# Attention with a relative bias and a snake MoE layer: two shared PSUM banks, MoE blocks entered inside a head pair, and a new order

## The chip, the cores and the metric

The kernel runs on one core of a Trainium2 chip. Its engines are TensorE (PE in the profile: matmuls and transposes, with PEld for the loading of weights), VectorE (DVE), ScalarE (ACT: exponentials and sines), GpSimd (POOL: here it issues loads that change the type from float32 to float16) and SyncE (SP: it issues transposing and plain transfers). Each engine works through its own list of instructions in order; an instruction waits until what it needs is there, and everything behind it on that engine waits too. The metric is device time in microseconds; lower is better.

## The reference

Batch element by batch element (8), head by head (8), over 576 positions with 64 numbers a head:

```python
scores = scale * q @ k.T  + bias_table[bucket(|i - j|)]
attn   = exp(scores - max) ; attn = attn / (sum(attn) + 1e-9)
x      = (attn @ v), heads side by side          # 4608 tokens x 512
h      = x @ w_in                                # 4608 x 2048
g      = h + sin(alpha * h) ** 2 / (alpha + 1e-9)
out    = g @ w_out                               # 4608 x 512, float32
```

The bias depends only on the distance of two positions and is constant from distance 128 on.

## The kernel before, in words

**Attention.** An element's heads are taken in four pairs (`attn_pair`). Scores are made transposed, keys on partitions. A pair has five tiles of 128 x 1024 in PSUM, each of two banks: one "X" tile for the last 64 keys and the last 64 queries, and four "T" tiles, named T(element).(pair).(w)(half), for 256 keys by 256 queries of both heads. For elements 0 and 1 an "S" tile follows after pair 1; from element 2 on it comes first, and it holds the last 64 keys against the last 64 queries of all heads. ScalarE takes the exponential of each tile into `u` (L567, some 0.94 us each); VectorE multiplies a band by a mask of exponentials of the bias (`band`, `band_x`, L736 to L744, L659, L661), since the bias is a constant outside the band. The numerators and the denominators come from matmuls of `u` with `v` and a column of ones (`av_task`, L680, L684): two groups per pair, the first of two, the second of three units. `norm` (L694, L695) divides into `xp`, and a transposing transfer on SyncE's queue (L775) writes `xT`, features on partitions.

**MoE.** The 4608 tokens are taken in nine blocks of 512 (`moe_in`). A block has eight parts `in b.d` (L800: eight matmuls of 512 columns each into a two-bank tile), each followed by two sines on ScalarE (L810), a square (L817) and two fused products on VectorE (L824), which read the tile again and write `g`. Then come four output tiles `mo b.a` (L857), each of four pieces of four matmuls that add up in one bank, an eviction on VectorE (`ev`, L873) and a store.

**PSUM.** The eight banks are three two-bank tiles `big` for scores and MoE parts, one bank `av` for numerators and the small masks, and one bank `mo` for the MoE outputs and for the transposes of keys and queries. Only the last two blocks put every second output into `av`.

**Masks.** The mask matrix `m2` has three blocks of 128 columns per head; `mask` makes each by 64 small matmuls (L476) and an exponential (L480). `masks_tail` makes `mt` from it.

**Loads.** Keys and queries of elements 0 and 1 come by GpSimd in their natural layout and are transposed by TensorE (`load_nat`, `turn`, L400 and L394): element 0 in runs of six rows, element 1 in `natural_chunk` loads, 128 positions of all heads each, with a tail. From element 2 on they are staged in DRAM as float16 (L242), transposed on SyncE's queue (L249), and the last 64 keys are put into `kL` (L433), which `S` and `X` tiles use. GpSimd's queue holds, for element 1: keys and queries, `w_in`, `v`, `w_out`.

**Order.** No order is written down: every piece of work is a task with an engine, a planned duration, what it depends on, rings of buffers and a priority; `_Plan.run` steps through planned time and emits, whenever an engine is free, the ready task with the lowest priority number. The planned times decide nothing but the order in which instructions stand on each engine; on the chip semaphores hold. Score tiles go in batches of two; `"big"` and `"ACT"` are sequences in the order of the code, so where `moe_in` is called decides where a block's parts stand among the scores: for element t, block t - 1 is called after pair 1. The output pieces `mo` fill in between (priority 2).

Of the kernel before, what the change touches and what calls it, by code (L numbers as in the profile page):

```python
# [25 lines left out]
class _Ring:  # L26
# [6 lines left out]
    def can(self, k):  # L33
# [11 lines left out]
        return end  # L45

# [14 lines left out]
class _Plan:  # L61
# [46 lines left out]
    def run(self):  # L108
# [9 lines left out]
        while left:  # L118
            moved = False
            nxt = None  # L120
            for e, lst in engs.items():
# [13 lines left out]
                if best is not None:  # L135
# [8 lines left out]
                    for ring, users in best.rings:  # L144
                        ring.users.append(users)
# [11 lines left out]
        return order  # L157


@with_exitstack  # L160
def kernel(
# [11 lines left out]
    nc = tc.nc  # L173
# [26 lines left out]
    for g in range(4):  # L200
# [31 lines left out]
    big, avr, mor = _Ring(3), _Ring(1), _Ring(1)  # L232
    ur, usr, sr, sqr, gr, xr, outr, rr = (
        _Ring(NU), _Ring(2), _Ring(NS), _Ring(NS), _Ring(NG), _Ring(NX), _Ring(NO), _Ring(4))

# [38 lines left out]
    def natural_chunk(src, t, kind, c):  # L274

        def emit():
            nc.gpsimd.dma_start(
                out=rows_of(t)[:, 5 * kind + c, :].rearrange("p (h d) -> p h d", d=D),
                in_=bass.AP(tensor=src.tensor, offset=src.offset + t * H * S * D + 128 * c * D,
                            ap=[[D, 128], [S * D, H], [1, D]]))  # L280
        return emit
# [89 lines left out]

    T_kT = [[None] * NP for _ in range(T)]
# [7 lines left out]
    def turn(t, p):  # L380

        for kind in range(2):
# [3 lines left out]
            def e_pe(kind=kind, cell=cell, first=first):  # L386

                bank = "av" if first else "mo"
                s = cell["t"] = ps.tile([128, 512], F32, name=bank, tag=bank, bufs=1).bitcast(F16)
# [17 lines left out]
            def e_cp(kind=kind, cell=cell, first=first):  # L407
# [7 lines left out]
                else:  # L415
                    nc.vector.tensor_copy(out=dst, in_=src)
            users = []
            a = add("PE", 0.6, e_pe, deps=T_nat[t][p][kind] + [t_sp0], prio=-0.5 if t else -2 if p == 0 else 0,
                    rings=[(avr, users)] if first else [(mor, users)], mode="full",
                    name=f"turn{t}.{p}.{kind}")  # L420
# [19 lines left out]
    def load_nat(t):  # L440
# [3 lines left out]
        def one(emit, dur, lat):  # L444
            first = not made
            made.append(add("GQ", dur, emit, lat=lat, seq="GQ",
                            rings=[(gr, nat_users[t])] if first else []))
            return made[-1]
        if t == 0:
            for h0, n, lat in ((0, 2, 4.0), (2, 2, 5.0), (4, 4, 6.0)):  # L450
                got = [[one(natural(src, t, kind, h0, n), 0.5 * n, lat)] for kind, src in kq]
                for p in range(h0 // 2, (h0 + n) // 2):
                    T_nat[t][p] = got
        else:
            got = [[one(natural_tail(src, t, kind), 0.7, 4.0)] for kind, src in kq]
            for kind, src in kq:
                got[kind] += [one(natural_chunk(src, t, kind, c), 0.9, 5.0) for c in range(4)]
            for p in range(NP):
                T_nat[t][p] = got

    load_nat(0)
    T_v[0] = add("GQ", 5.0, load_v(0), deps=[t_dve0], lat=6.0, seq="GQ")

# [29 lines left out]

    T_mt = []
    t_al = add("SP", 0.5, pre_sp2, deps=T_m2, lat=6.0)
    t_alpha = add("DVE", 0.4, pre_alpha, deps=[t_al])

    def masks_tail():

        for pp in range(2):  # L500
            cell = {}

            def g_mm(pp=pp, cell=cell):
                av = ps.tile([128, 512], F32, name="av", tag="av", bufs=1)
# [8 lines left out]
            def g_cp(pp=pp, cell=cell):  # L513
# [3 lines left out]
            a = add("PE", 0.4, g_mm, deps=list(T_m2), prio=-1, rings=[(avr, users)],  # L517
                    mode="full")
            b = add("DVE", 0.5, g_cp, deps=[a], prio=-1, name=f"mt.{pp}")
# [7 lines left out]
    def later_loads(t):  # L527
        pre_k = last_qk[t - 2] if t >= 2 else []
        pre_v = last_av[t - 2] if t >= 2 else [t_dve0]
        def w_ins():  # L530
            for j in range(4):
                T_win.append(add("GQ", 2.5, w_in_load(j), lat=6.0, seq="GQ"))

        def kqs():
            if t < TN:
                load_nat(t)
                return
            a = add("GQ", 4.0, stage(k, staged_k, t), lat=2.5, seq="GQ")
            b = add("GQ", 4.0, stage(q, staged_q, t), lat=2.5, seq="GQ")
# [7 lines left out]
        def v_s():  # L547
            T_v[t] = add("GQ", 5.0, load_v(t), deps=pre_v, lat=3.0, seq="GQ")

        def w_outs():  # L550
            for i in range(4):
                T_wout.append(add("GQ", 2.5, w_out_load(i), lat=6.0, seq="GQ"))
# [398 lines left out]
```

## Time and profile before

| what | us |
| --- | --- |
| median of three runs (406.03, 407.64, 407.49) | 407.49 |
| the profiled execution's own time | 406.59 |
| its span, from the first to the last instruction | 404.6 |
| TensorE busy | 375.5 |
| VectorE busy | 289.5 |
| ScalarE busy | 270.1 |
| GpSimd busy | 82.6 |
| mean granted TensorE clock | 0.987 of full |

The profile shows one execution. A line of the timeline gives the start, the busy time, the engine, the source line, the operation with its tiles, how many instructions were merged, and in brackets the idle time of that engine before it with what ended it. A line of waits gives who waited for whom: the total, how often, the longest. In the stretches, the columns are the length and the busy time of each engine with its number of instructions, then the granted clock.

### The profile page before, as it was taken

The page shows a single profiled execution, that of the slowest core. Times are in us where ns is not written, and L with a number is a line of the kernel's source. Part 1 is how long each engine was busy: PE and PEld are TensorE (multiplying, and loading weights), DVE is VectorE, ACT ScalarE, POOL GpSimd, SP SyncE. Part 2 cuts the span into 40 slices and gives each one's busy share as a digit, 9 for nine tenths or more (in the row PEclk, how much of TensorE's full clock was granted, in tenths as well). Part 3 has the DMA queues.
Part 4 walks back from the last instruction along what each step waited for, and adds up shares of the span by engine and source line. Part 5 has one row for each costly group of instructions (what it writes and reads, how often), then busy time and mean ns, then how long its engine had stood idle before and what let it go on. Part 6 is the DMA issues. An engine that isn't in the chain of part 4 may idle for free.

```text
span 404.6 us, 9103 instructions
## 1 busy us (share of the span) xinstructions
PE 375.5 (93%) x3816; PEld 202.9 (50%) x3816; DVE 289.5 (72%) x618; ACT 270.1 (67%) x333; POOL 82.6 (20%) x88
## 2 busy tenths in 40 slices
PE   6788599989999999999999999999999998999996
PEld 5465353555446554555456545654565454444442
DVE  4587469666976698659956896779666964699811
ACT  4688656977588847895788668866888583566200
POOL 8772634053002600080008000400000000000000
PEclk9699899999999999999999999999999999999999
DMA  9999999999933998199919991981021103000121
GB/s 128 137 180 159 168 178 158 157 161 156 145 82 57 153 154 110 45 145 140 132 56 114 150 139 56 113 145 42 28 64 40 32 38 86 26 0 2 52 79 78
DMA packets 167180, 41.27 MB, mean 102 GB/s; under 512 B 158308, under 2 KB 162020, under 8 KB 167140
## 3 DMA queue, kind: packets, MB, share of 16 engines
q0 software_dynamic: 106816, 18.36, 60.9%
q1 hardware_dynamic: 60180, 22.17, 31.7%
q8 instruction: 30, 0.49, 0.5%
q10 hardware_dynamic: 144, 0.17, 0.2%
q14 instruction: 10, 0.08, 0.1%
HBM read 36.88 MB, written 16.52 MB: 132 GB/s over the span
## 4 chain that ended last, share of the span: by engine, by line
PE 49%; DVE 25%; DMA 11%; ACT 10%; issue 5%; SPq 0%; POOL 0%; ACTq 0%; DVEq 0%; POOLq 0%
PE mo L857 20%; DVE g L824 11%; PE big L800 11%; DMA xT<-xp 8%; ACT u L567 7%; DVE sq L817 5%; PE av L684 5%; PE big L725 3%; PE av L857 3%; DVE outs L873 3%; DVE xp L695 2%; ACT s L810 2%; DMA kL<-kT 2%; DVE u L736 2%; PE av L680 1%
## 5 line engine op out<-in xcount | busy, mean ns | idle before, releaser
L567 ACT ACTIVATE u<-big 128x1024 f16<-128x1024 f32 x160 | 153.3, 1026 | 32.2 <-PE big L725 20.6
L810 ACT ACTIVATE s<-big,alphaT 128x512 f16<-128x512 f32 x144 | 90.6, 684 | 67.2 <-PE big L800 67.0
L800 PE MATMUL big<-xT,w_in 128*128 128x512 f16 x576 | 132.1, 379 | 1.9 <-DMA xT<-xp 1.2
L857 PE MATMUL mo<-w_out,g 128*128 128x512 f16 x512 | 127.6, 380 | 6.7 <-DVE outs L873 6.0
L824 DVE SCALAR_TENSOR_TENSOR g<-sq,inv_a,big 128x512 f16<-128x512 f16 x144 | 101.2, 744 | 2.3
L800 PEld LDWEIGHTS <-w_in 128*128 128x128 f16 x576 | 55.8, 98 | 69.1 <-issue 4.3
L857 PEld LDWEIGHTS <-g 128*128 128x128 f16 x576 | 52.0, 97 | 71.4 <-issue 17.1
L736 DVE TENSOR_TENSOR u<-u,m 128x1024 f16<-128x1024 f16 x64 | 44.1, 689 | 24.7 <-ACT u L567 24.7
L817 DVE TENSOR_TENSOR sq<-s 128x1024 f16<-128x1024 f16 x72 | 49.3, 684 | 15.9 <-ACT s L810 15.9
L298 POOL DMA_DIRECT2D v<-in_v_dram x32 | 29.4, 1008 | 151.0 <-PE av L684 151.0
L684 PE MATMUL av<-v,u 128*128 128x65 f16 x1280 | 55.4, 194 | 0.0
L684 PEld LDWEIGHTS <-u 128*128 128x128 f16 x1280 | 50.9, 98 | 4.1
L725 PE MATMUL big<-qT,kT 64*128 64x256 f16 x512 | 42.2, 278 | 0.6 <-ACT u L567 0.3
L680 PE MATMUL av<-vt,u 128*128 128x130 f16 x128 | 28.6, 224 | 7.4 <-DMA vt<-in_v_dram 4.0
L695 DVE TENSOR_TENSOR xp<-av,rden 128x256 f16<-128x256 f32 (+1 forms) x64 | 31.4, 491 | 3.8 <-DMA xT<-xp 1.6
L873 DVE COPY outs<-mo 128x512 f32<-128x512 f32 x32 | 21.9, 686 | 14.1 <-PE mo L857 13.9
L725 PEld LDWEIGHTS <-kT 64*128 64x128 f16 x512 | 19.8, 96 | 13.4 <-issue 10.5
L680 PEld LDWEIGHTS <-u 128*128 128x128 f16 x128 | 12.4, 97 | 15.6 <-DVE xp L695 6.1
L694 DVE RECIPROCAL rden<-av 128x4 f32<-128x4 f32 (+1 forms) x64 | 11.8, 184 | 11.9 <-PE av L684 11.8
L744 DVE TENSOR_TENSOR u<-u,m 128x256 f16<-128x256 f16 x32 | 9.3, 290 | 14.9 <-ACT u L567 14.9
L242 POOL DMA_DIRECT2D staged_q<-in_q_dram x6 | 16.1, 2681 | 2.4 <-DMA staged_q<-in_q_dram 2.4
L857 PE MATMUL av<-w_out,g 128*128 128x512 f16 x64 | 14.5, 379 | 0.0
(64 smaller groups left out, 187.3 us busy)
## 6 DMA issues: line engine op xcount, KB each, us to landing
out_dram<-outs SPq DMA_DIRECT2D x36, 256.0 KB, 2.3
v<-in_v_dram POOLq DMA_DIRECT2D x32, 128.0 KB, 6.0
staged_k<-in_k_dram POOLq DMA_DIRECT2D x6, 576.0 KB, 14.2
staged_q<-in_q_dram POOLq DMA_DIRECT2D x6, 576.0 KB, 20.0
w_in<-in_moe_w_in_dram POOLq DMA_DIRECT2D x4, 512.0 KB, 10.6
w_out<-in_moe_w_out_dram POOLq DMA_DIRECT2D x4, 512.0 KB, 14.4
vt<-in_v_dram POOLq DMA_DIRECT2D x16, 32.0 KB, 5.8
g<-in_k_dram POOLq DMA_DIRECT2D x4, 128.0 KB, 4.0
```

The source lines that it names most:

```text
L567: nc.scalar.activation(out=cell["u"][:, 0:exp_cols], in_=cell["s"][:, 0:exp_cols], func=AF.Exp, scale=0.125)
L680: nc.tensor.matmul(out=av[:, o:o + 130], lhsT=tail, rhs=vt_[:, p, 0:130], start=True, stop=True, skip_group_check=True)
L684: nc.tensor.matmul(out=av[:, o + 65 * a_:o + 65 * a_ + 65], lhsT=bl(a_, c), rhs=vv[:, c, hA + a_, 0:65], start=False, stop=True, skip_grou ...
L695: nc.vector.tensor_tensor(out=ap(x, 128 * q0, [[64, 2 * n], [1, 64]]), in0=ap(av, 0, [[65, 2 * n], [1, 64]]), in1=ap(r, 0, [[1, 2 * n], [0 ...
L725: nc.tensor.matmul(out=s[:, 512 * a_ + 256 * ci:512 * a_ + 256 * ci + 256], lhsT=kT[r, p, 128 * c:128 * c + 128], rhs=qT[r, p, 256 * w:256 ...
L736: nc.vector.tensor_tensor(out=io, in0=io, in1=m2[:, hA:hA + 2, :], op=ALU.mult)
L800: nc.tensor.matmul(out=cell["h"][:, 512 * i:512 * i + 512], lhsT=w_in16[:, j, 128 * f:128 * f + 128], rhs=xT[:, j, 512 * b:512 * b + 512], ...
L810: nc.scalar.activation(out=cell["s"][:, 512 * i:512 * i + 512], in_=cell["h"][:, 512 * i:512 * i + 512], func=AF.Sin, scale=alphaT[:, f:f ...
L817: nc.vector.tensor_tensor(out=cell["sq"], in0=cell["s"], in1=cell["s"], op=ALU.mult)
L824: nc.vector.scalar_tensor_tensor(out=gcell["g"][:, f, :], in0=cell["sq"][:, 512 * i:512 * i + 512], scalar=inv_a[:, f:f + 1], in1=cell["h" ...
L857: nc.tensor.matmul(out=cell["mo"][:, :], lhsT=gcell["g"][:, f, 128 * a_:128 * a_ + 128], rhs=w_out16[:, f, :], start=(f == 0), stop=(f == ...
L873: nc.vector.tensor_copy(out=cell["o"], in_=cell["mo"][:, :])
```

## The change

1. The banks `av` and `mo` become two banks `sm0` and `sm1` that numerators, MoE outputs, turns and masks share. `_Banks` gives a task the bank that the plan frees first.
2. A MoE block is entered inside pair 2 of the next element, after its third T tile (`between`), instead of after pair 1; the second output tile of a block need not follow the first ("free"); the third piece of a block's last output (and so the fourth) is held until the next block's first part is issued (`HOLD`).
3. Element 1's keys and queries come in `natural_head` loads, one head and 512 positions each, in two groups of pairs; its `v` goes ahead of them.
4. The mask block of distances of the other sign is made by transposing the block made before it, in place of 64 matmuls and an exponential.
5. Priorities stand in a table `P`, with new values; the first product of a block goes ahead of the others in dependence. Loads get a model of their own in the plan. alpha's load no longer waits for the masks.

As built, SyncE's queue has the transposes of element 1's pairs 0 and 1 ahead of `kT`, `qT` and `kL` of element 2, where before one of them stood between `kT` and `qT`; TensorE's list has pair 1's two turns before `X0.0`, and pieces of `mo b.0` and `mo b.1` mixed in block 0 alone. VectorE's list has the square and the two products of a part as an unbroken run, save for one `norm` a block, after the fourth part (for block 0, the fifth), and in block 1 also one `ev`.

```diff
+class _Banks:
+    def __init__(self, n):
+        self.last = [[] for _ in range(n)]
...
+    def take(self, users):
+        free = [(e, i) for i, e in enumerate(map(self._free, self.last)) if e is not None]
+        i = min(free)[1]
+        self.last[i] = users
+        return i
...
+P = {
+    "moe0": 2, "moe": 2, "where": 3, "av0": 1.6, "av1": 1.9, "mo": 2, "band": 1.3, "bandh": 0.6,
+    "bandX": 0.6, "bandS": 2.0, "norm0": 1.2, "norm1": -0.5, "sq": 0.5, "stt": -0.8, "ev": 1.1,
+    "turn": 0, "turn1": 2.0, "where0": 3, "free": 1, "batch": 2
+}
+HOLD = {(3, 2): 0}
+LOADS = ("v_s", "kq_a", "kq_b", "w_ins", "w_outs")
...
-    big, avr, mor = _Ring(3), _Ring(1), _Ring(1)
+    big, small = _Ring(3), _Banks(2)
...
+    def small_bank(cell):
+        name = f"sm{cell['task'].bank}"
+        return ps.tile([128, 512], F32, name=name, tag=name, bufs=1)
...
-                out=rows_of(t)[:, 5 * kind + c, :].rearrange("p (h d) -> p h d", d=D),
-                in_=bass.AP(tensor=src.tensor, offset=src.offset + t * H * S * D + 128 * c * D,
-                            ap=[[D, 128], [S * D, H], [1, D]]))
+                out=rows_of(t)[:, 5 * kind:5 * kind + 4, D * h:D * h + D],
+                in_=bass.AP(tensor=src.tensor, offset=src.offset + (t * H + h) * S * D,
+                            ap=[[D, 128], [128 * D, 4], [1, D]]))
...
+    def mask_turned():
+        cell = {}
+        def e_pe():
+            s = cell["s"] = small_bank(cell).bitcast(F16)
+            for h in range(H):
+                nc.tensor.transpose(out=s[:, 128 * h:128 * h + 128], in_=m2[:, h, 128:256],
+                                    identity=i_sb)
+        def e_cp():
+            nc.vector.tensor_copy(out=m2[:, :, 256:384],
+                                  in_=cell["s"].rearrange("p (h y) -> p h y", h=H))
...
-        for load in ((kqs, w_ins, v_s, w_outs) if t == 1 else (kqs, v_s)):
-            load()
+        parts = dict(kq_a=kq_a, kq_b=kq_b, w_ins=w_ins, w_outs=w_outs, v_s=v_s)
+        for part in ([parts[n] for n in LOADS] if t == 1 else (kqs, v_s)):
+            part()
...
-            a = add("PE", 0.29 * n, emit, deps=deps + [T_v[t]], prio=1, rings=[(avr, users)],
+            a = add("PE", 0.29 * n, emit, deps=deps + [T_v[t]], prio=P["av1" if q0 else "av0"], rings=[(small, users)],
...
+                if between is not None and 2 * w + half + 1 == between[0]:
+                    between[1]()
...
+            for o, ob, od_ in held:
+                if (ob, od_) == (b, d):
+                    o.deps.append(a)
...
-                st = add("DVE", 0.66, e_stt(i), deps=[sq, t_alpha], prio=0.4,
+                st = add("DVE", 0.66, e_stt(i), deps=[sq, t_alpha] + stts[:1], prio=P["stt"],
...
-                if last is not None:
+                if piece or (last is not None and (not P["free"] or a_ != 1)):
                     deps.append(last)
                 users = []
-                last = add("PE", 0.87, e_mo, deps=deps, prio=2,
-                           rings=[] if piece else ([(avr, users)] if late else [(mor, users)]),
+                hold = HOLD.get((a_, piece))
+                last = add("PE", 0.87, e_mo, deps=deps, prio=P["mo"],
+                           rings=[] if piece else [(small, users)],
                            name=f"mo{b}.{a_}", mode="full")
+                if hold is not None and b < NBLK - 1:
+                    held.append((last, b + 1, hold))
...
-            mask(0, 256)
+            mask_turned()
...
-            attn_pair(t, p, sc)
+            at = (P["moe0"], P["where0"]) if t == 1 else (P["moe"], P["where"])
+            blk = (lambda: moe_in(t - 1)) if t and p == at[0] else None
+            if blk and not at[1]:
+                batch["open"] = None
+                blk()
+            attn_pair(t, p, sc, (at[1], blk) if blk else None)
...
-            if p == (1 if t == 1 else 1) and t >= 1:
-                moe_in(t - 1)
```

## The prediction

> **What bounds the kernel now.** I read the page first (busy shares, slices), then the busy time of each engine by stretch, then TensorE's waits in one element's stretch, then the timeline of the first 85 us with SyncE's and GpSimd's queues.
>
> ```profile
> span 404.6 us, 9103 instructions
> PE 375.5 (93%) x3816; PEld 202.9 (50%) x3816; DVE 289.5 (72%) x618; ACT 270.1 (67%) x333; POOL 82.6 (20%) x88
> PE   6788599989999999999999999999999998999996
> DMA  9999999999933998199919991981021103000121
> ```
>
> TensorE is the bound; the transfers are busy in nine tenths or more for the first 111 us (11 slices of 10.1 us). So there are two stages: a start held by transfers, and a long stretch held by TensorE.
>
> ```profile
> 82.30:404.60 322.30, 310.82 (x2811) 161.58 (x2811) 233.75 (x475) 213.87 (x267) 41.72 (x38) 1.00 0.75 87
> 167.44:209.55 42.11, 41.10 (x418) 22.16 (x417) 32.27 (x70) 31.99 (x40) 9.23 (x8) 1.00 1.13 114
> 45.00:50.00 5.00, 4.23 (x55) 3.15 (x56) 2.17 (x7) 2.40 (x4) 4.96 (x4) 0.66 1.23 198
> ```
>
> Columns: stretch, length, busy PE, PEld, DVE, ACT, POOL, granted clock, DMA share, GB/s. Between two `S` tiles (one element of the batch; the `S` of elements 4 and 5 start at 167.44 and 209.55) TensorE idles 1.0 of 42.1 us. From 82.3 to the end it idles 11.5 us; 3.8 of them are the last eviction and store (390 to the end), which stay. So 7.7 us can be won there at most.
>
> ```profile
> PE mo L857 <- DVE outs L873: 0.8, 3, 0.3
> PE av L680 <- DVE xp L695: 0.2, 1, 0.2
> ```
>
> TensorE's waits from 140 to 180 us: the one MoE bank waits three times for its eviction, the one numerator bank once. This is the whole idle time of an element.
>
> ```profile
> 45.77 0.24 PE L680 MATMUL av<-vt,u 128*128 128x130 f16 x1 [3.96 <-DMA vt<-in_v_dram]
> 50.59 4.69 PE L800 MATMUL big<-xT,w_in 128*128 128x512 f16 x21 [0.48 <-DMA xT<-xp]
> 82.27 0.28 PE L608 MATMUL big<-qT,kL 128*128 128x64 f16 x4 [1.19 <-DMA kL<-kT]
> ```
>
> ```profile
> 60.64 5.94 SPq L249 DMA_TRANSPOSE kT<-staged_k  x1
> 66.68 1.43 SPq L775 DMA_TRANSPOSE xT<-xp  x1
> 68.22 6.91 SPq L249 DMA_TRANSPOSE qT<-staged_q  x1
> 75.17 1.37 SPq L433 DMA_DIRECT2D kL<-kT  x2
> ```
>
> The start has three waits on transfers: element 1's `v` (3.96), block 0's `xT`, and element 2's `kL` (1.19), which SyncE's queue reaches only at 75.17 and which lands 7.0 us later.
>
> **The change, part by part.**
>
> *Start, TensorE and ScalarE.* One mask loses 64 of the 192 small matmuls (128 took 3.46, so 1.75 us) and one exponential of 1.02 on ScalarE; it gets 8 transposes (5 took 0.52, so 0.8) and a VectorE copy that the trace lacks: between 0.45 (576 columns, plain) and 0.76 (576, strided), I take 0.8 for 1024. `X0.0` moves ahead of the mask, but behind both turns of pair 1. The second of these needs `q` of heads 2 and 3 (issued 3.29; such a load landed in 4.5). So the first exponential comes at about 11 us, not 14.47. Cover: this is worth nothing at the end unless the transfers follow.
>
> *`v` of element 1 ahead of its keys and queries.* The 3.96 us wait at 41.8 goes. Keys and queries come 4.9 us of GpSimd issue later (the `v` rows: 3.57 and 1.29). Eight loads of 128 KB at 0.89 become sixteen of 64 KB. Such a load is not in the trace; the nearest rows are the 64x8x64 tail, as many runs of 64 numbers (0.69), and the 128x8x64 load, twice as many (0.89). I take 0.70: 11.2 us against 7.1, at most 14.2. Past GpSimd's ring waits (2.5 us before 15 us, as now) the last goes out at about 30, lands near 35, and is used near 37. `w_in`, behind them on GpSimd's queue, goes out at 30 to 33 instead of 21 to 23 and lands at 43 to 46; its first user comes near 46. Between 20 and 31 the transfers are fed at 64 KB per 0.70, where the 128 KB loads fed at 128 KB per 0.89; with some 4 us of work queued this loses 0.6 to 4 us of transfer time for all that follows: I take 2.
>
> The sixteen small loads are where the Trainium skill speaks against the change: DMA: Bandwidth & Descriptors, section Bandwidth, asks for large transfers and lists 0.95 us for 64 KB. By that figure sixteen cost 15.2 us instead of my 11.2, 4 us more, and by it the estimate below would lose up to that much. No row here shows a 64 KB load of this shape.
>
> *Block entry.* MoE block b enters after pair 2's third row tile instead of after pair 1: four score tiles, and for block 0 the numerators of pairs 0 and 1, come ahead of it. For block 0, 34 tiles at 0.94 and two `S` at 0.39 take 32.8 us of ScalarE from 11: 44. `xT` of pair 3, issued near 35, takes the 10 us it took now. So block 0 starts near 46, not 50.6. From block 0 to `S2` it was 50.6 to 82.3 less 1.2 of wait: 30.5; moved ahead are about 1.3 of scores and 1.8 of numerators, and a MoE piece of 0.86 is pulled in from behind. That is 28 to 30, so TensorE reaches `S2` at 74 to 78.
>
> *But `S2` needs `kL`.* The loads ahead of it are the same bytes. SyncE's queue now holds `kT`, `qT`, `kL` in a row, with no `xT` between (it saves 1.43), and the transfers lose 2: 82.3 − 1.4 + 2 gives 82.9, bounds 80 to 85. I take 82.5. So the start's whole gain turns into a wait of 4 us or more on `kL`. Behind it in TensorE's order stand the scores, so ScalarE starves as well. At `S2` 0.9 us of MoE work more is done, and the time is 0.2 later: +0.7.
>
> After the 3.96 us gap the granted clock was 0.66 for 5 us, with 4.23 of them busy: 4.23 × 0.34 = 1.4 us lost. The gap of 1.19 cost no clock. The new gap is of the first kind: −1.4. The Trainium skill, TensorE: Matmul & The Clock Gate, section HAM oscillation — how this bites in real kernels, warns of gaps over some 3.4 us. Row and rule agree on which of the two gaps costs; by the rule alone, halved speed over 3.4 us would be 1.7.
>
> *Middle, the two shared banks and the new order.* Walked by rows for one element, from `in b.0` at 0 (a block's part 1.73, a MoE piece 0.86, numerators 0.59 or 0.89, square 0.64, the two products 1.41, a table load 1.28, a sine pair 1.27): the first square at 3.9, products done at 6.0, 8.0, 10.1, 12.1, then the numerators' division (0.6), 14.8, 16.8, 18.9, 20.9. TensorE comes to parts 3 to 7 at 6.7, 9.2, 11.0, 12.7, 15.3: each at least 0.5 after the product it needs. The next score pair comes at 18.75 and needs 18.9: 0.15 of wait. After that `mo b.1` comes 0.65 after `ev b.0`, and the numerators find the other bank free 1.3 us earlier or more. Without waits the element is 41.0 (busy 41.1). I take 0.3 of idle (0.15, and as much for what the walk misses) for six elements, and 0.4 for the tail, where one wait of 0.78 on an eviction stood: 2.2 left of 7.7, +5.5. Bounds: nothing left (+7.7), and the margins gone: 0.65 to 1.3 us per allocation, below.
>
> The `xT` waits of TensorE (1.2 in three) are among the 7.7; the later entry removes them. Ahead of block 7 five or six MoE pieces (0.86 each, 5.2) cover the last `xT` (division 0.8, issue 1.2, landing 2.6). In the middle `kL` lands at `in b.0` + 22 and `S` comes at + 27: a margin of 5, down from 8. Element 3 is the tightest.
>
> *Sum.* +0.7 − 1.4 + 5.5 = 4.8 faster: span 399.8, and 406.59 − 4.8 = 401.8 for the profiled execution. The three runs' median lies 0.9 above that execution; I predict 402.5.
>
> **Rivals.**
> 1. *The start's gain arrives.* `kL` is not tied to the bytes ahead of it: the sixteen loads cost less, and the transposes, freed from `xT`, are faster. For it: transposes took 2.3 to 2.9 each where little else moved (262.8 to 268). Against: the transfers are full until 111. `S2` at 78, no lost clock: 4.5 + 1.4 more, 396.5.
> 2. *Transfers later.* GpSimd needs 0.89 per small load, `w_in` and `kL` are 6 to 8 us later: `S2` at 88.5 instead of 82.5: 408.5.
> 3. *The waits change name.* The order is written by a plan that charges 0.66 for a product (0.70 here) and 0.61 for an eviction (0.69); if evictions and divisions come as late as banks are now, the idle of 1.0 an element stays, six times 0.7 more than I take: 402.5 + 4.2 = 406.7.
> 4. *Slower: the shared banks.* Products now rank above evictions and divisions on VectorE. If in every element one numerator group or MoE group finds both banks held while a square and two products (2.05) stand ahead of the eviction, six elements idle 12.3 where I take 1.8: 413. It decides from a lateness of 0.65 (the walk's margin); at 1.1 us an element the gain is gone, at 1.5 it is slower. For it: four kinds of work share what two kinds had each to themselves. Against: the margins above, by rows.
>
> **How the numbers follow.** What a measurement can tell from no change is 0.5%, 2.0 us. Forecast 0.46 (its own range 399 to 405.4), rival 1 0.18, rival 2 0.09, rival 3 0.11, rival 4 0.16. Faster: 0.46 + 0.18 + 0.06 (parts of 2 and 3) = 0.70. Same: 0.14, the rest of 2 and 3. Slower: 0.16. Range: 395.5 (rival 1, with half of the 2.2 left in the middle gone too) to 409.5, which leaves rival 4 and a few hundredths below.
>
> **What would show it.** No wait on `vt`; block 0's first matmul near 46; the wait on `kL` at `S2` grows to 4 us or more, with a clock under 1 after it; TensorE's waits on evictions fall from 6.0 us to under 2; elements of 41.2 to 41.6 from `S` to `S`. Wrong if: `S2` comes before 80 (rival 1) or after 86 (2); waits on evictions and divisions stay near 1 us an element (3) or pass 2 (4).

## The result, and the profile after

The changed kernel takes 401.64 us (median of four runs, 399.94 to 402.88) against 407.12 for the kernel before (median of four): a ratio of 0.9866, 95% interval 0.9822 to 0.991. It is faster, by 1.3%. 402.5 was forecast; the profiled execution, forecast at 401.8, took 402.1, and its span is 400.0.

The page of the changed kernel: span, busy time, and the slices of TensorE, its granted clock and the transfers.

```profile
span 400.0 us, 9012 instructions
PE 374.4 (94%) x3760; PEld 202.4 (51%) x3760; DVE 288.5 (72%) x619; ACT 269.5 (67%) x332; POOL 87.4 (22%) x96
PE   6798499759999999999999999999999999999996
PEclk9879799969999999999999999999999999999999
DMA  9999999999971997299929992992122013000122
```

TensorE's row has nines from the tenth slice to the last but one. The start still has its holes, in the fifth (4) and the ninth (5).

The busy time by stretch, changed kernel: from `S2` to the end, then the first element after `S2`, then the fourth. Columns as before: stretch, length, PE, PEld, DVE, ACT, POOL, granted clock, DMA share, GB/s.

```profile
84.12:400.00 315.88, 310.12 (x2807) 161.30 (x2807) 232.50 (x474) 214.44 (x267) 41.72 (x38) 0.99 0.75 89
84.12:126.42 42.30, 41.04 (x404) 22.05 (x405) 30.61 (x65) 31.76 (x39) 9.24 (x8) 0.94 1.25 124
208.13:248.98 40.85, 40.76 (x422) 21.88 (x419) 32.06 (x69) 32.16 (x40) 9.23 (x8) 1.00 1.16 117
```

An element takes 40.85 with 0.09 idle, where it took 42.1 with 1.0. From `S2` to the end it is 315.88 against 322.34: 6.46 won. Idle time gave 5.7 of it (11.49 to 5.76), busy time the other 0.7. `S2` itself comes later, at 84.13 instead of 82.27, so the start lost 1.86 us; 6.46 − 1.86 = 4.60, the difference of the spans.

TensorE's waits of the changed kernel from 85 to 125 us; from 125 to 350 us there is none of 0.2 us or more, and none on an eviction anywhere:

```profile
PE sm L942 <- DVE g L908: 0.6, 2, 0.3
PE big L805 <- ACT u L644: 0.5, 1, 0.5
```

The kernel before had these, from 85 to 350:

```profile
PE mo L857 <- DVE outs L873: 5.7, 19, 0.8
PE av L680 <- DVE xp L695: 1.0, 6, 0.2
PE big L800 <- DMA xT<-xp: 0.7, 2, 0.6
```

And the start, from the changed kernel's timeline: a division on VectorE, a numerator group, block 0, `S2`.

```profile
46.97 0.42 DVE L774 TENSOR_TENSOR xp<-sm,rden 128x256 f16<-128x256 f32 x1 [6.46 <-DMA xT<-xp]
48.25 0.29 PE L759 MATMUL sm<-vt,us 128*128 128x130 f16 x1 [5.83 <-DVE us L695]
51.09 5.16 PE L884 MATMUL big<-xT,w_in 128*128 128x512 f16 x22
84.13 0.37 PE L687 MATMUL big<-qT,kL 128*128 128x64 f16 x4 [6.63 <-DMA kL<-kT]
```

The wait of 3.96 on element 1's `v` is gone. (The first exponential of scores comes at 10.06 instead of 14.47, and a new wait of 1.33 stands at 17 us, on element 0's `vt`.) But at 48 us stands a new one of 5.83. Read upward: VectorE's division into the sixth `xp`, that of element 1's second pair, waited 6.46 for one of the three buffers, which `xT` of element 0's third pair had not yet left (that transposing transfer took 15.8 us to land). VectorE works in order, so the product `us` behind it was late, and TensorE waited for `us`. Block 0 begins at 51.1. At `S2` TensorE is ready at 77.5 and waits 6.63 for `kL`.

The stretches right behind that wait, in the changed kernel; the granted clock is the first figure after POOL's bracket:

```profile
84.13:86.00 1.87, 1.87 (x16) 0.83 (x17) 0.29 (x1) 1.09 (x2) 0.00 (x0) 0.50 1.41 243
86.00:88.00 2.00, 2.00 (x12) 0.62 (x11) 0.36 (x2) 0.66 (x2) 0.00 (x0) 0.50 2.14 156
88.00:90.00 2.00, 2.00 (x32) 1.69 (x31) 1.05 (x3) 1.59 (x2) 0.22 (x1) 0.71 1.10 76
```

Half clock until about 89.2 (0.71 over the last two us), and TensorE busy all the while: 5.03 us at half, some 2.5 us of its time lost. The first element takes only 1.45 more than the others (42.30 against 40.85) because it holds 13 MoE pieces of 0.86 instead of 16; it also has 1.16 more of idle time.

So there are two questions. Which part of the change emptied the middle of waits? And why did the start give nothing, although TensorE came to `S2` 3.6 us earlier (77.5 against 81.1)?

### The profile page after: what moved, and what is told of

Its sections match the earlier page's. It is cut to its first block, busy times and chain, and to the rows that moved or that the text cites. A ratio compares the mean times of both kernels' runs of the same rounds, so it can differ in the third digit from the quotient of the medians.

```text
span 400.0 us, 9012 instructions
## 1 busy us (share of the span) xinstructions
PE 374.4 (94%) x3760; PEld 202.4 (51%) x3760; DVE 288.5 (72%) x619; ACT 269.5 (67%) x332; POOL 87.4 (22%) x96
## 4 chain that ended last, share of the span: by engine, by line
PE 52%; DVE 25%; ACT 8%; DMA 7%; issue 4%; POOL 2%; SPq 0%; DVEq 0%; ACTq 0%; POOLq 0%
PE sm L942 25%; DVE g L908 16%; PE big L884 8%; DVE sq L901 7%; PE sm L763 7%; PE big L805 7%; ACT u L644 4%; DMA xT<-xp 4%; PE sm L759 3%; ACT s L894 2%; ACT L894 2%; DMA vt<-in_v_dram 2%; DMA kL<-kT 2%; PE big L729 1%; PE big L714 1%
## 5 line engine op out<-in xcount | busy, mean ns | idle before, releaser
L644 ACT ACTIVATE u<-big 128x1024 f16<-128x1024 f32 x160 | 153.4, 1035 | 30.7 <-PE big L805 28.9
L942 PE MATMUL sm<-w_out,g 128*128 128x512 f16 x576 | 140.5, 382 | 0.6 <-DVE g L908 0.6
L884 PE MATMUL big<-xT,w_in 128*128 128x512 f16 x576 | 130.3, 380 | 0.2 <-DVE g L908 0.2
L343 POOL DMA_DIRECT2D v<-in_v_dram x32 | 28.3, 900 | 153.9 <-PE sm L763 148.1
L763 PE MATMUL sm<-v,u 128*128 128x65 f16 x1280 | 57.7, 197 | 0.2
L763 PEld LDWEIGHTS <-u 128*128 128x128 f16 x1280 | 52.9, 100 | 2.7 <-DVE u L818 0.3
L962 DVE COPY outs<-sm 128x512 f32<-128x512 f32 x36 | 24.7, 687 | 19.9 <-PE sm L942 19.7
L774 DVE TENSOR_TENSOR xp<-sm,rden 128x256 f16<-128x256 f32 (+1 forms) x64 | 31.4, 491 | 8.6 <-DMA xT<-xp 6.5
L759 PE MATMUL sm<-vt,u 128*128 128x130 f16 x128 | 29.2, 228 | 1.6 <-DMA vt<-in_v_dram 1.3
L759 PEld LDWEIGHTS <-u 128*128 128x128 f16 x128 | 12.5, 98 | 12.9 <-issue 6.3
L773 DVE RECIPROCAL rden<-sm 128x4 f32<-128x4 f32 (+1 forms) x64 | 11.8, 185 | 7.6 <-PE sm L763 7.6
L287 POOL DMA_DIRECT2D staged_k<-in_k_dram x6 | 13.6, 2260 | 4.7 <-DMA staged_k<-in_k_dram 4.5
```

What stands on the lines that cost most here:

```text
L287: nc.gpsimd.dma_start(out=dst.ap()[t].rearrange("s (h d) -> s h d", h=H), in_=src[t].rearrange("h s d -> s h d"))
L644: nc.scalar.activation(out=cell["u"][:, 0:exp_cols], in_=cell["s"][:, 0:exp_cols], func=AF.Exp, scale=0.125)
L759: nc.tensor.matmul(out=av[:, o:o + 130], lhsT=tail, rhs=vt_[:, p, 0:130], start=True, stop=True, skip_group_check=True)
L763: nc.tensor.matmul(out=av[:, o + 65 * a_:o + 65 * a_ + 65], lhsT=bl(a_, c), rhs=vv[:, c, hA + a_, 0:65], start=False, stop=True, skip_grou ...
L774: nc.vector.tensor_tensor(out=ap(x, 128 * q0, [[64, 2 * n], [1, 64]]), in0=ap(av, 0, [[65, 2 * n], [1, 64]]), in1=ap(r, 0, [[1, 2 * n], [0 ...
L884: nc.tensor.matmul(out=cell["h"][:, 512 * i:512 * i + 512], lhsT=w_in16[:, j, 128 * f:128 * f + 128], rhs=xT[:, j, 512 * b:512 * b + 512], ...
```

## The experiments: the middle

Each kernel was timed beside the kernel before on the same chip; ratios are to that one.

### The shared banks alone

```diff
-    big, avr, mor = _Ring(3), _Ring(1), _Ring(1)
+    big, small = _Ring(3), _Banks(2)
...
-                           rings=[] if piece else ([(avr, users)] if late else [(mor, users)]),
+                           rings=[] if piece else [(small, users)],
```

The kernel before with the two shared banks and nothing else.

> The kernel before, with one part of the change: the two shared small banks (the plan then gives its own order to the pieces); entry, loads, masks and priorities as before. Theory (the shared banks carry the middle's gain): TensorE's waits on evictions and on divisions, 1.0 us an element, go; elements of 41.0 to 41.3 us from S to S instead of 42.1; S2 where it was, about 82.3; 401 to 403 us. Rival (the entry and the priorities carry it): the waits come back under the same or other names, elements stay above 41.8, 406 to 407.5 us.

411.31 against 406.69, ratio 1.0112 (1.0074 to 1.015): slower. TensorE's waits from 85 to 350:

```profile
PE sm L892 <- DVE g L860: 4.3, 12, 0.5
PE sm L715 <- DVE xp L730: 1.0, 6, 0.2
PE big L836 <- DMA xT<-xp: 0.4, 1, 0.4
```

The waits on evictions are gone, as the sharing promises. In their place the output pieces wait for the products `g` (4.3 us in 12). This is the rival "the waits change name", in this kernel: the four middle elements take 170.17, before it was 169.38. The loss is in the start, where `S2` comes at 87.35, 5.1 later; the end gives some 2 of it back. Banks alone win nothing in the middle.

### The change without the shared banks

```diff
-    big, small = _Ring(3), _Banks(2)
+    big, small_av, small_mo = _Ring(3), _Banks(1, 0), _Banks(1, 1)
...
-            a = add("PE", 0.29 * n, emit, deps=deps + [T_v[t]], prio=P["av1" if q0 else "av0"], rings=[(small, users)],
+            a = add("PE", 0.29 * n, emit, deps=deps + [T_v[t]], prio=P["av1" if q0 else "av0"], rings=[(small_av, users)],
...
-                           rings=[] if piece else [(small, users)],
+                           rings=[] if piece else [(small_av if b >= T - 1 and a_ % 2 == 1 else small_mo, users)],
```

> The changed kernel with numerators and masks in one bank and MoE outputs and turns in the other, as before; all else as changed. Theory (shared banks): waits on evictions return, 0.8 to 1.0 us an element, elements of 41.7 to 42 us, 406 to 408 us. Rival (order): elements stay at 40.9 to 41.1 us, 401 to 403 us. As this order puts the pieces of a block's outputs further apart, a third outcome is that the outputs fall behind their block and the tail grows instead.

437.86 against the kernel before, ratio 1.0799 (1.0723 to 1.0876), span 436.1, elements of about 43.9. TensorE's waits from 85 to 350:

```profile
PE sm L943 <- DVE outs L963: 12.7, 8, 2.1
PE big L806 <- DVE g L909: 6.0, 4, 1.7
PE big L885 <- DVE g L909: 4.7, 3, 1.7
```

Such a wait was 0.3 on average in the kernel before, and 0.8 at most; now it is up to 2.1, since the products rank above evictions on VectorE and the lone bank must wait for both. Of the 36.1 us that the span grows over the changed kernel's, 24.9 are idle time behind `S2` (30.7 against 5.8) and 10.6 busy time; the clock stood at half for some 24 us there. With its own bank each, the new order loses what it wins and more: the order needs the second bank.

### The old priorities in the changed kernel

```diff
-    "moe0": 2, "moe": 2, "where": 3, "av0": 1.6, "av1": 1.9, "mo": 2, "band": 1.3, "bandh": 0.6,
-    "bandX": 0.6, "bandS": 2.0, "norm0": 1.2, "norm1": -0.5, "sq": 0.5, "stt": -0.8, "ev": 1.1,
-    "turn": 0, "turn1": 2.0, "where0": 3, "free": 1, "batch": 2
+    "moe0": 2, "moe": 2, "where": 3, "av0": 1, "av1": 1, "mo": 2, "band": 1, "bandh": 1,
+    "bandX": 1, "bandS": 1, "norm0": 0, "norm1": 0, "sq": 0.5, "stt": 0.4, "ev": 0.8,
+    "turn": 0, "turn1": -0.5, "where0": 3, "free": 0, "batch": 2
...
-HOLD = {(3, 2): 0}
+HOLD = {}
```

> The changed kernel (shared banks, late entry, new loads, turned mask) with the priorities of before, no held pieces and no free second output. The banks alone gave elements of 42.4 us, with waits on the products. Theory (banks and priorities carry the middle only together: shared banks take away the eviction waits, products ranked first take away the waits on products): elements of 41.6 to 42.4 us, waits on products of 0.7 us or more an element, 405 to 409 us. Rival (banks and late entry suffice): elements of 40.9 to 41.1 us, 401 to 403 us.

406.63 against 407.37, ratio 0.9974 (0.9956 to 0.9991); span 404.7. The elements take 41.5 to 41.6. TensorE's waits from 85 to 350:

```profile
PE big L805 <- DVE g L908: 2.1, 3, 0.7
PE sm L942 <- DVE g L908: 1.8, 6, 0.3
```

Again it is the products that are late. The priorities (with the hold and the freed second output) are worth 0.7 us an element, and 1.1% of the whole (ratios 0.9974 and 0.9866).

### The blocks entered after pair 1 again

```diff
-            blk = (lambda: moe_in(t - 1)) if t and p == at[0] else None
+            blk = None
...
+            if p == 1 and t >= 1:
+                moe_in(t - 1)
```

> The changed kernel with MoE blocks entered after pair 1 again. Theory (the late entry is needed so that neither xT nor the products are waited for): waits of 0.3 to 0.8 us an element, elements of 41.2 to 41.7 us, 403 to 406 us. Rival (the entry does nothing for the middle): elements of 40.9 us, 400 to 402.5 us; the start would be held by kL of element 2 as in the changed kernel, S2 at 82 to 85.

426.78 against 407.37, ratio 1.0476 (1.0433 to 1.0518): slower by far more than either theory gave. An element takes 44.34. Here are two lines of TensorE's timeline, and then the stretches behind them; the same pair of gaps comes in four elements.

```profile
158.29 0.39 PE L805 MATMUL big<-qT,kT 64*128 64x256 f16 x4 [1.44 <-DVE g L908]
160.89 1.89 PE L942 MATMUL sm<-w_out,g 128*128 128x512 f16 x4 [2.21 <-DVE xp L774]
```

```profile
160.00:162.00 2.00, 1.11 (x3) 0.43 (x4) 1.93 (x8) 0.84 (x1) 0.00 (x0) 0.50 0.00 0
162.00:164.00 2.00, 2.00 (x11) 0.58 (x10) 0.40 (x1) 0.64 (x1) 0.00 (x0) 0.50 0.42 82
164.00:166.00 2.00, 2.00 (x6) 0.76 (x5) 0.58 (x2) 1.29 (x2) 0.00 (x0) 0.50 0.00 0
166.00:168.00 2.00, 2.00 (x27) 1.10 (x26) 0.00 (x0) 0.33 (x1) 0.00 (x0) 0.81 0.00 0
```

VectorE was busy for 3.93 of the 4.00 us from 156.9 to 160.9: products, which rank first, and only then the division `xp` that the output piece waits for, since it is to have that bank. The early entry puts a block's products and a division in one place. The two waits cost 3.65 an element, and then the clock is at half for 6.8 us (159.9 to 166.8).

**What the four say.** Shared banks, priorities and entry are one thing. Products that rank first make the scores and parts come in time; they make evictions and divisions late; two banks that any work may take hide that lateness; and the later entry keeps a division from falling due behind a block's products (that last is read from the one timeline above). Take one away and TensorE waits again: elements of 43.9, 41.6, 44.3, against 40.85 with all. The lengths 43.9 and 44.3 understate the loss, because most of these elements hold 12 MoE pieces instead of 16 and the rest comes at the end; the spans have it all. Alone in the old kernel the banks are worth less than nothing. Each edit also makes the plan write the whole order anew, so these are kernels without a part, not one order with a part taken out. The turned mask was not taken out by itself.

## The experiments: the start

### No `kL` for element 2

```diff
-    TN = 2
+    TN, TK = 2, 3
...
-            corners(t, [c] + pre_k)
+            if t >= TK:
+                corners(t, [c] + pre_k)
...
-                         (T_kL[t] if t >= TN else T_kT[t]) + T_qT[t], f"S{t}",
+                         (T_kL[t] if t >= TK else T_kT[t]) + T_qT[t], f"S{t}",
```

Element 2 takes its last keys straight from `kT`, in the form that elements 0 and 1 have.

> The changed kernel; element 2 takes the last 64 keys straight from kT, as elements 0 and 1 do, so that it needs no kL. Theory (the wait of 6.6 us at S2 is for kL, and the cold clock after it costs 1.45): S2 then waits for qT only, whose transpose is issued from 69.2 to 76.9 and lands 5 to 8 us later, between 78 and 83; S2 at 79 to 83 instead of 84.1, gain 1.5 to 6, 395.5 to 400 us. Rival (the start is bound by bytes, not by kL): qT lands as late as kL, no gain, 401 to 402 us.

399.3, ratio 0.9814 (0.9779 to 0.985), span 396.7. `S2` comes at 80.79, 3.34 earlier than in the changed kernel's trace, and now waits 5.94 for `qT`. The wait on `kL` was on the path; without it, the transfer ahead of it in SyncE's queue is the one that ends last.

Not all of the 3.34 is the edit's. Up to 80 us the lists of TensorE, VectorE, ScalarE and GpSimd are those of the changed kernel, instruction by instruction, and SyncE's is up to `kT` and `qT`. Yet `kT` goes out 1.64 earlier, first the changed kernel's line, then this one's:

```profile
63.47 5.61 SPq L294 DMA_TRANSPOSE kT<-staged_k  x1
61.83 5.65 SPq L294 DMA_TRANSPOSE kT<-staged_k  x1
```

The wait of 5.83 at 48 us is absent here too: `xT` of element 0's third pair took 5.3 us instead of 15.8, block 0's first matmul stands at 41.66, and its fourth, which needs pair 3's `xT`, at 47.51 instead of 51.99. So two traces of the same instructions can differ by 1.6 us at `kT` and by more at block 0. Differences of that size between single traces do not show what an edit does. In the changed kernel's trace `kL` landed 1.3 after `qT`; that is an estimate of what this edit is worth. The two ratios' intervals (0.9779 to 0.985, and 0.9822 to 0.991) overlap.

### Element 2's staging ahead of `w_out`

```diff
-LOADS = ("v_s", "kq_a", "kq_b", "w_ins", "w_outs")
+LOADS = ("v_s", "kq_a", "kq_b", "w_ins")
...
-        for part in ([parts[n] for n in LOADS] if t == 1 else (kqs, v_s)):
+        for part in ([parts[n] for n in LOADS] if t == 1 else (kqs, w_outs, v_s) if t == 2 else (kqs, v_s)):
```

> The changed kernel; the keys and queries of element 2 are staged ahead of w_out instead of behind it. Theory (the bytes ahead of the staging set when kL lands): 2 MB of w_out took some 10 to 12 us of transfers, so kT, qT and kL come 8 to 12 us earlier, the wait at S2 (6.6 us) and the cold clock after it (1.45 us) go; w_out lands at about 65 instead of 59, just ahead of the pieces that need it; 394 to 396 us. Rival (what is moved behind waits instead): the first MoE outputs wait for w_out by 3 to 6 us, 398 to 402 us.

397.7, ratio 0.9777 (0.974 to 0.9813), span 395.9. `kT` of element 2 is issued at 53.33 instead of 63.47, but `kT` and `qT` take 9.1 and 9.3 us on SyncE's queue instead of 5.6 and 7.7, so `kL` is issued at 71.85 instead of 76.95 and `S2` comes at 80.77, after a wait of 3.77.

### Both at once

The two edits above together.

> Both cures of the start together: element 2's staging ahead of w_out, and no kL for element 2. Each alone put S2 at 80.8 instead of 84.1, once held by qT, once by kL behind qT. Theory (a chain of transposes in one queue, and each cure shortens another part of it): S2 at 76 to 78.5, with a wait under 2 us and no cold clock after it; 393 to 395.5 us. Rival (both cures remove the same wait): S2 at 80 to 81, 397 to 399 us.

396.36 against 407.37, ratio 0.9705 (0.9645 to 0.9766), span 394.5: `S2` at 79.08, after 2.79 on `qT`.

### Element 1's loads as before

```diff
-LOADS = ("v_s", "kq_a", "kq_b", "w_ins", "w_outs")
+LOADS = ("kq_a", "w_ins", "v_s", "w_outs")
...
+            got = [[T_tail[0]], [T_tail[1]]]
+            for kind, src in kq:
+                got[kind] += [one(natural_chunk(src, t, kind, c), 0.9, 0.9) for c in range(4)]
...
-            load_nat(t, range(0, 2))
+            load_nat(t, range(0, NP))
```

> The changed kernel with element 1's loads as before: keys and queries in eight loads of 128 KB and two tails, then w_in, v, w_out. Theory (v ahead of the keys wins time only up to S2, and S2 is held by kL): the wait on v of 4 us returns, the wait at S2 shrinks by as much; the sixteen small loads no longer hold back what follows, so S2 at 81 to 84 instead of 84.1; 399 to 402 us. Rival (the order of the loads is worth its wait): 403 to 406 us.

401.42 against 407.37, ratio 0.9854 (0.9808 to 0.99): the same as the changed kernel. `S2` comes at 84.40, just later than the theory's range. The wait on `v` of 4 us does not return; TensorE waits 7.90 at 39 us for a division instead. This looks as if the sixteen small loads cost nothing and `v` first won nothing. But the two kernels come to `kT` by different ways. In the changed one SyncE's queue has done its sixth `xT` at 53.4 and then waits 10.0 us for the staged keys. With the old loads there is no such wait: the sixth `xT` holds the queue until 63.17 and `kT` goes out behind it, at 63.27. So one limit could hide the other, and the last two experiments take the transposes away.

### Element 0's `xT` made by TensorE

```diff
+        if t == 0:
...
+            def x_pe():
+                s = xc["s"] = small_bank(xc).bitcast(F16)
...
+                    nc.tensor.transpose(out=s[:, 128 * c:128 * c + n], in_=x[0:n, c, :],
+                                        identity=i_sb[0:n, 0:n])
+            def x_cp():
+                nc.vector.tensor_copy(out=xT[:, p, 0:S], in_=xc["s"][:, 0:S])
```

> The changed kernel; element 0's four xT transposes are made by TensorE (five transposes of 128 columns a pair, 0.53 us, and a copy of 0.45 on VectorE) in place of the transposing transfers. Theory (kL came 1.9 us later than before because two xT transposes instead of one stand ahead of the staging on full transfers; each takes 10 us and more there): block 0 starts at 45 to 48 instead of 51.1, TensorE waits on no xp buffer, staging lands 2 to 5 us earlier, S2 at 79 to 82.5; 396.5 to 400 us. Rival (the loads alone set when kL lands): S2 at 83.5 to 84.5 with a longer wait on kL, 400.5 to 402 us.

399.4 against 406.11, ratio 0.9832 (0.9807 to 0.9858). Two lines of TensorE's timeline:

```profile
46.14 5.34 PE L905 MATMUL big<-xT,w_in 128*128 128x512 f16 x24
80.98 0.40 PE L687 MATMUL big<-qT,kL 128*128 128x64 f16 x4 [8.25 <-DMA kL<-kT]
```

Without the late transposing transfers block 0 begins at 46.14. TensorE is ready for `S2` at 72.7, and waits 8.25 for `kL`: of the 5 us that block 0 gained, none counts at the end. What counts is that `kT` went out at 60.94 and `S2` came 3.15 earlier. Measured against the trace of "No `kL` for element 2", `kT` is only 0.9 earlier, and the ratio's interval overlaps that of the changed kernel, so what the edit is worth at the end is not settled.

### All three

Both edits of the start and this one.

> All three cures of the start together: staging of element 2 ahead of w_out, no kL for element 2, element 0's xT by TensorE. With the first two S2 was at 79.1, after a wait of 4.2 us on xT at block 0, 2.4 on w_out and 2.8 on qT. Theory (transfers bound the start, so each transposing transfer less brings all behind it forward): block 0 at 44 to 47, S2 at 73 to 77, 389.5 to 393.5 us. Rival (qT's chain of two transposes of 9 us in SyncE's queue is bound by the queue): S2 at 78 to 79.5, 394.5 to 397 us.

396.27 against 406.11, ratio 0.9751 (0.9725 to 0.9777), span 394.5: no more than the two edits together. `kT` goes out at 49.58 and occupies SyncE's queue for 14.95 us, `qT` for 8.26; `S2` still waits 3.06 for `qT`, at 78.84. The chain of the two transposes in SyncE's queue ends no earlier; whether the queue or the transfers beside it hold it, no run separates.

### Only element 1's first two `xT` made by TensorE

```diff
-        tr = add("SP", 1.4, xtr, deps=norm_done, lat=3.0)
...
+        if t == 1 and p < 2:
...
+            xa = add("PE", 0.6, x_pe, deps=norm_done, prio=1.0, rings=[(small, xu)], mode="full",
+                     name=f"xt{t}.{p}")
...
+            tr = add("DVE", 0.45, x_cp, deps=[xa], prio=0, name=f"xt{t}.{p}c")
...
+        else:
+            tr = add("SP", 1.4, xtr, deps=norm_done, lat=3.0)
```

These two stand ahead of `kT` in the changed kernel's queue; before the change one of them did.

> The changed kernel with one edit: xT of element 1's pairs 0 and 1 is made by five TensorE transposes and a VectorE copy each; element 0's four stay transposing transfers on SyncE's queue. What holds kT of element 2 in the changed kernel: its trace shows SyncE's queue idle for 10.0 us (53.4 to 63.5) until the staged keys land, so the two transposes of element 1 ahead of kT should not matter. Theory A (the staged keys land at 63.5 because the sixteen small loads feed the transfers less from 20 to 35 us: 6.59 MB moved from 20 to 60 us, against 6.86 before, 0.27 MB or 1.7 us at 157 GB/s): kT is still issued at 62 to 64, S2 stays at 83 to 84.3, profiled span 398.5 to 400.5. Theory B (the two more transposes on the queue, by their own transfer time, cost the 2 us): kT at 60.5 to 61.5, S2 near 81.5, span 397 to 398.3.

398.09 against 406.86, ratio 0.9792 (0.9768 to 0.9816). SyncE's queue, and `S2`:

```profile
24.10 11.03 SPq L857 DMA_TRANSPOSE xT<-xp  x4
60.06 5.76 SPq L294 DMA_TRANSPOSE kT<-staged_k  x1
```

```profile
80.64 0.37 PE L687 MATMUL big<-qT,kL 128*128 128x64 f16 x4 [3.99 <-DMA kL<-kT]
```

Theory A falls, by the times too: the interval lies just clear of the changed kernel's (0.9822 to 0.991). The staging load was issued at the same time as in the changed kernel (37.01 and 37.05), and yet its keys landed 3.4 us earlier than in that trace, and 1.8 earlier than in the trace of "No `kL` for element 2", which has the same transposes ahead. So the two transposes, though the queue was idle behind them, had delayed it, by some 1.8 to 3.4 us together.

### The old loads, with these two `xT` made by TensorE

The edits of the last experiment and of "Element 1's loads as before" together.

> The kernel with element 1's loads as before (e3_loads_back), and with xT of element 1's pairs 0 and 1 by TensorE and VectorE as in e13. In e3_loads_back kT was issued at 63.27 without any wait for the staged keys, directly behind the sixth transpose on SyncE's queue, which ended at 63.17. Theory A (the small loads cost about 1.7 us of transfer time, and with the old loads it is SyncE's queue that eats the gain): with the two transposes gone from ahead of kT, kT is issued at 59.5 to 61.5 as before the change (60.64), and S2 comes at 80.5 to 82.3, 1.5 to 3 us before e13's; span 396.5 to 398.5. Theory B (the load order is worth nothing either way): kT and S2 within 0.7 us of e13's.

396.94 against 406.86, ratio 0.9769 (0.9742 to 0.9795), span 394.3.

```profile
59.13 5.71 SPq L294 DMA_TRANSPOSE kT<-staged_k  x1
```

```profile
79.54 0.28 PE L697 MATMUL big<-qT,kL 128*128 128x64 f16 x4
```

`kT` goes out 0.93 earlier than with the small loads, `S2` comes 1.10 earlier. That lies between the two theories (1.5 to 3, and within 0.7), and below the 1.6 by which two traces of the same instructions differ; the intervals of the two ratios overlap. So a cost of the load order is not shown; if there is one, it is nearer 1 us of transfer time than 2. And `S2` does not wait at all here. TensorE gets there only at 79.5, held up by a wait of 6.8 at 38 us on a division that had to wait for `xT` to leave its `xp`; so there is no cold clock behind `S2`, and the next element takes 41.06 instead of 42.3 to 42.6. In these two traces that is why it ends 2.5 us before the last kernel, with `S2` only 1.1 earlier.

## Why the prediction was right, and where its steps were off

**The sum.** The forecast was +0.7 − 1.4 + 5.5 = 4.8 off the profiled span; it was 4.6. That it fits within 0.2 is luck, for no term had the right size. The start lost 1.0 (1.86 later, with one MoE piece of 0.86 more done) where it was to win 0.7: 1.7 worse. The cold clock cost some 2.5 instead of 1.4: 1.1 worse. The middle won 8.1 (6.46 − 0.86 + 2.5) instead of 5.5: 2.6 better. (The median, too, has a slip: 401.8 and the 0.9 make 402.7, not 402.5.)

**Middle, +5.5.** The mechanism was right, and rivals 3 and 4 did not come. After `S2` idle time fell by 5.7, with 2.0 left besides the last eviction and store (5.76 − 3.8), where 2.2 was forecast. The walk by rows expected 0.3 of idle an element and lengths of 41.2 to 41.6; it was 0.09, and 40.85. The term was too small because busy time shrank as well, which I had not priced; so "7.7 us can be won there at most" was no bound. Over four middle elements, from 124.65 before and from 126.43 after:

```profile
124.65:294.03 169.38, 164.70 (x1666) 88.64 (x1665) 129.30 (x277) 128.09 (x157) 32.49 (x30) 1.00 0.98 106
```

```profile
126.43:289.83 163.40, 163.03 (x1671) 87.54 (x1668) 128.25 (x276) 128.64 (x157) 32.49 (x30) 1.00 1.04 110
```

Of 5.98 won, 4.31 is idle time and 1.67 busy time, for the same matmuls to within five. Busy time of a pipelined engine is not a fixed sum of durations: where waits break the stream, it also holds time that goes when they go. That is how I read it; no run takes it apart.

Rival 4 asked from what lateness shared banks turn slower, and put the danger in the sharing. The danger was the other way round: the new priorities without sharing cost 8%. Its mechanism, evictions behind the products, is the one seen there.

**Start: block 0 near 46.** It came at 51.1. The step that failed is "`xT` of pair 3, issued near 35, takes the 10 us it took now". It was issued at 35.63, took 15.5 and landed at 51.14; in the six other kernels that issue it at 33 to 35 us it took 13.2 to 14.6. In this trace a second such transfer, that of pair 2, took 15.8 and held an `xp` buffer, VectorE and TensorE in turn. With those transfers gone, block 0 began at 46.14. From block 0 to `S2` 28 to 30 us was forecast; it was 26.4 here (26.6 in the kernel without those transfers). So TensorE's arrival at `S2`, forecast at 74 to 78 and measured at 77.5, is right by two misses. Neither counted at the end, because `S2` waits for `kL` in either case.

**Start: `S2` needs `kL`, 82.5.** The mechanism was right (a wait of 4 us or more; it was 6.63, and `S2` comes earlier in the kernels that loosen it), but `S2` came at 84.13, late by 1.6. Two traces of the same instructions differ by as much at `kT`, so one trace cannot say how far the forecast was off. What the experiments do show is a term left out of "82.3 − 1.4 + 2": I counted moving an `xT` from behind `kT` to ahead of it only as a saving of 1.43 on the queue. Measured: `kT` went out 2.83 later than before, and `kL` 1.78 later. So the queue saved about 1.0 between them. But the transposes moved ahead delay the staged keys, two of them by 1.8 to 3.4; the one that was moved by 0.9 to 1.7, if they share it evenly, which no run tests. The load order, taken at 2, is nearer 1 and not shown to be more than nothing. As an estimate, 0.9 to 1.7, and 0 to 0.9, less 1.0, is −0.1 to 1.6, against 1.86 measured for `S2`. Rival 2, with 0.89 for a small load and `S2` at 88.5, did not come.

The Trainium skill's rule in DMA: Bandwidth & Descriptors, section Bandwidth, weighed in the prediction, spoke against the small loads. The page lists 0.95 us for 64 KB, but as the time in which the DMA engines are busy, without the issuing; the prediction set it against times of issue, which are another thing. GpSimd's queue shows the issue of two of these loads in 1.53 to 1.63 us, some 0.8 each: more than the 0.70 taken. In sum, with the later `w_in`, the order costs at most about 1 us where it can be seen, and nothing as the change was built.

**Cold clock, −1.4.** The mechanism was right, the size was not. The price came from the gap of 3.96, after which TensorE worked at half for 3.4 us; after 6.63 it worked at half for 5.03, some 2.5 us. The last experiment agrees: there the clock is full behind `S2`, and the element is busy for 40.28 with 15 MoE pieces, where the changed kernel's is busy for 41.05 with 13. Two pieces are 1.73, so the difference is 2.5. Rival 1 failed for the reason given: the transfers stay full to 110 us, and `S2` waits.

## What to carry to other kernels

Where TensorE waits for one bank, look at the bank, the order on the engine that frees it and the place where other work enters as one thing: here the kernel without any one of the three lost most or all of the gain, and with all of them an element's idle time went from 1.0 us to 0.09. Where the start is held by transfers, find the one that ends last before making the work ahead of it faster (block 0 came 5 us sooner in one kernel, and none of that reached the end). And price a transfer that is moved ahead of it by what it takes from the loads in flight, not by its turn on its queue alone: two transposes delayed the load by some 1.8 to 3.4 us on a queue that stood idle behind them. Before a difference between two traces is put down to an edit, look how far two traces of the same instructions differ: here by 1.6 us where `kT` goes out.

## What was not expected of the hardware

The clock. In these traces it is either full or half, and before the last matmul half lasts 3.41 us or a multiple of it. After the gap of 6.63 us it was at half until 89.2, which was expected in kind. But with the blocks entered after pair 1 it fell to half after two gaps of 1.44 and 2.21 us with only 0.39 us of matmuls between them, from 159.9 to 166.8 us; in the kernel with its own banks the same happened after 1.66 and 2.13 with 0.51 between. And one gap alone was enough in "Both at once", before `S2`:

```profile
79.08 0.31 PE L683 MATMUL big<-qT,kT 64*64 64x64 f16 x8 [2.79 <-DMA qT<-staged_q]
```

After these 2.79 us, with busy stretches on both sides, the clock was at half from 80.1 to 83.5; with the banks alone it was from 39.4 to 42.8, after one gap of 1.85 at 39.1. The gap of 1.19 us before `S2` in the kernel before cost no clock, nor did one of 1.47 there at 38.3. The Trainium skill, TensorE: Matmul & The Clock Gate, section HAM oscillation — how this bites in real kernels, speaks of idle gaps over some 3.4 us. Here shorter ones cost the clock, and the measurement decides: 2.79 and even 1.85 were enough, 1.47 was not. Whether the length of the gap alone decides, no run shows. In those four elements of the entry experiment the mean clock was 0.87 and then 0.92, which adds to the 3.65 of waits.

The best of these kernels stand at 396 to 397 us. The version with the staging ahead of `w_out` and no `kL` for element 2 took 396.36 against 407.37 (0.9705, 0.9645 to 0.9766), the one with all three edits 396.27 against 406.11; both beat the kernel before and the changed one.
